# Attention and gated feed-forward on one core: the last 512 queries as two chunks of 256, two key tiles to a score bank, loads and first normalisations reordered

## The chip, the core and the metric

The kernel runs on one core of a Trainium2 chip. A core has five engines that work from queues of their own and meet through semaphores: TensorE (PE, matmuls; its weight loads are shown apart as PEld), VectorE (DVE), ScalarE (ACT), GpSimd (POOL) and SyncE (SP), which here issues the transfers between the main memory and the on-chip memory. Matmuls write to eight score and work banks of 512 float32 per partition; every result is copied out of a bank by ScalarE or VectorE. The metric is the time of one execution on the device, in microseconds (us). Below 0.2% a difference can't be told from none here.

## What is computed

A transformer block on 2048 tokens of width 512, in bfloat16: layer norm, attention with 32 heads of width 16, the output projection and the residual, then layer norm, a gated feed-forward of width 1792 and its residual.

```python
qkv = (x @ wqkv).reshape(B, S, 3, H, Dh).transpose(2, 0, 3, 1, 4)   # of the normalised x; H = 32, Dh = 16
scores = einsum("bhqd,bhkd->bhqk", q, k) * Dh ** -0.5
o = einsum("bhqk,bhkd->bhqd", softmax(scores), v)
h = x + o.transpose(0, 2, 1, 3).reshape(B, S, D) @ wo
h2 = h + (gelu(hn @ w_gate) * (hn @ w_up)) @ w_down                  # hn: h normalised; gelu by tanh; F = 1792
```

## The kernel before, in words

The work is cut by queries into four chunks of 512 (`NCH`). A chunk has eight units (`NSLOT`), each of four heads; a unit runs over 16 key tiles of 128 (`NT`). The smallest piece is a score tile: one head group `g`, one key tile `kt`, 512 queries, which fills one bank. There are 32 units x 16 x 4 = 2048 of them (`TILES`), and they are taken in steps of three and two banks in turn (`SLOTS`, `STEPS`): 819 steps. A step is one set of score matmuls (`qk`; four heads side by side in the array, 32 rows each), then one exponential of ScalarE over the three or two banks (`exps`, L1153 by its helper), whose bfloat16 result goes to a ring of 30 tiles (`PT`). The value matmuls (`pv`) take four tiles at a time and add over the key tiles in one bank (`PVB`), 17 rows per head: 16 values and the denominator. After a unit, `ofin` copies that bank (L1342), transposes it (L1346), inverts the denominators (L1350) and writes the divided result by token (L1353).

When a chunk has its eight units, `post` (four query tiles of 128) transposes them (L1383), copies (L1385), multiplies by `wo`, adds the residual (L1392), takes statistics (L1396, L1397), forms the factor by a power on POOL (L1399, L1400), normalises (L1401) and transposes back (L1405, L1407). Then `gates`, `ups` and `downs` run the feed-forward in 14 blocks of 128 (`NFC`): 56 gate matmuls, 56 up matmuls of 512 columns each, and 56 down matmuls. Chunks 0 to 2 do this under the scores of the next chunk, and their gelu is made of three POOL operations (L1433, L1434, L1435), a tanh on ScalarE between two exponentials (L1441) and VectorE operations. Chunk 3 does it when no scores are left, with the gelu of ScalarE's table (`gelu_tail`, L1447). `check` tests all denominators on VectorE (L1498 to L1504) and sets a flag that could send the kernel to a second path; it isn't taken here.

At the start, `loads` issues the transfers on SP, in order: x of chunk 0 in two halves, the first 128 columns of keys and of queries of `wqkv`, x of chunk 1, values, and so on. `ln1` normalises chunk by chunk: statistics on VectorE (L1213, L1214; for chunk 1 sums on ScalarE, L1199 and L1201), the factor of four tiles by one power on POOL (L1217), then the normalisation of four tiles (L1222), on VectorE for chunk 0 and on POOL for the others. `ln1_T` transposes each tile (L1229) and copies it (L1236, or L1234 on ScalarE). `proj_kq` and `proj_v` make keys, queries and values, and their results are copied by VectorE (L1260, L1270, L1282) and one by ScalarE (L1267).

What sets the order is a planner (`Sched`), run when the kernel is built: each piece of work is a stream with a due time (`prio`), each operation has an assumed duration, and the planner emits, engine by engine, the operation that can start first. On the chip each engine then runs its list strictly in that order. `fill` puts matmuls of zeros (L1513, L1523) where TensorE would pause, by a running count of columns owed (`RATE`, `OWED`); `warm` does so before the first scores (L1510).

## Time and profile before

| | |
|---|---|
| median of 3 runs | 1063.62 us (1062.66 to 1064.13) |
| profiled execution, its own time | 1062.85 us |
| its span, first to last instruction | 1061.1 us |
| granted TensorE clock, mean over the span | 0.990 |
| moved by all transfers | 14.96 MB |

A row of a timeline gives start and duration in us, engine, line, operation, result and operands, shapes and count, and in brackets the idle time before it with what ended it. A row of a group gives line, engine, operation and shapes, then busy us and the mean ns of one, then idle us before and what ended most of it. Rows of neighbouring instructions of one kind are merged, and their durations may overlap.

### The profile page before, as it was taken

The numbers are of one execution on the slowest core, as the hardware profiler recorded it, in microseconds if no ns is written. First come the engines' busy times: TensorE is split into PE (matmuls) and PEld (weight loads), VectorE is DVE, ScalarE is ACT, GpSimd is POOL, SyncE is SP. The second block draws the span as 40 slices with busy tenths as digits, with TensorE's granted clock in tenths as the row PEclk, the third lists the DMA queues.
The fourth block names the chain that finished last, engine by engine and source line by source line (L and its number), as shares of the span: only waits on it lengthen the run. The fifth ranks groups of instructions, "written<-read, shape, count | busy, mean of one in ns | idle before, by whom it ended". The sixth has DMA issues, their size and how long they took to land.

```text
span 1061.1 us, 15019 instructions
## 1 busy us (share of the span) xinstructions
PE 951.1 (90%) x6139; PEld 288.9 (27%) x6255; DVE 258.6 (24%) x462; ACT 971.7 (92%) x897; POOL 181.6 (17%) x191
## 2 busy tenths in 40 slices
...
DMA packets 12847, 14.96 MB, mean 14 GB/s; under 512 B 1760, under 2 KB 11744, under 8 KB 12768
## 3 DMA queue, kind: packets, MB, share of 16 engines
...
q14 instruction: 28, 0.23, 0.1%
...
## 4 chain that ended last, share of the span: by engine, by line
ACT 32%; PE 28%; issue 23%; POOL 12%; DVE 2%; ACTq 0%; POOLq 0%; DVEq 0%
ACT PT L1153 32%; PE pbank L1146 13%; PE pbank L1147 12%; POOL w_sb L1435 5%; POOL w_sb L1433 4%; POOL w_sb L1434 3%; PE pbank L1513 2%; POOL xn_sb L1222 1%; PE pbank L1346 1%; DVE g_sb L1431 0%; DVE QT L1270 0%; DVE stats_93 L1396 0%; ACTq L152 0%; PE pbank L1523 0%; DVE VA L1282 0%
## 5 line engine op out<-in xcount | busy, mean ns | idle before, releaser
L1153 ACT ACTIVATE PT<-pbank 128x1536 bf16<-128x1536 f32 (+1 forms) x819 | 934.1, 1406 | 21.4 <-PE pbank L1147 20.3
L1147 PE MATMUL pbank<-QT,KT 32*128 32x512 bf16 x2048 | 319.5, 386 | 69.6 <-ACT PT L1153 48.6
L1513 PE MATMUL pbank<-ones_bf,zero_bf 128*128 128x512 bf16 x743 | 226.3, 383 | 7.3 <-issue 7.0
L1147 PE MATMUL pbank<-PT,VA 128*17 128x512 bf16 x2048 | 201.0, 385 | 1.2 <-ACT PT L1153 0.4
L1147 PEld LDWEIGHTS pbank<-QT,KT 32*128 32x128 bf16 x2048 | 78.0, 91 | 380.8 <-ACT PT L1153 350.7
L1342 DVE COPY OA<-pbank 128x512 f32<-128x512 f32 x32 | 22.1, 691 | 501.6 <-PE pbank L1147 501.6
L1399 POOL TENSOR_SCALAR rstd_95<-mv_94 128x1 f32<-128x1 f32 x16 | 3.6, 224 | 793.4 <-DVE mv_94 L1397 791.0
L1513 PEld LDWEIGHTS pbank<-ones_bf,zero_bf 128*128 128x128 bf16 x811 | 57.0, 97 | 99.7 <-issue 84.6
L1147 PEld LDWEIGHTS pbank<-PT,VA 128*17 128x17 bf16 x2048 | 49.1, 87 | 118.1 <-issue 109.6
L1146 PE MATMUL pbank<-wd_sb,GUT 128*128 128x512 bf16 x215 | 56.4, 381 | 0.9 <-issue 0.8
L1435 POOL TENSOR_TENSOR w_sb<-w_sb,g_sb 128x512 f32<-128x512 f32 x42 | 56.1, 1336 | 3.5
L1433 POOL TENSOR_TENSOR w_sb<-g_sb 128x512 f32<-128x512 f32 x42 | 45.4, 1080 | 24.8 <-DVE g_sb L1431 24.8
L1442 DVE SCALAR_TENSOR_TENSOR w_sb<-w_sb,g_sb 128x512 f32<-128x512 f32 x42 | 34.8, 827 | 19.5 <-ACT w_sb L1441 19.3
L1146 PE MATMUL pbank<-xnT,wqkv_sb 128*128 128x512 bf16 x121 | 35.5, 394 | 1.0 <-issue 0.5
L1467 DVE SCALAR_TENSOR_TENSOR GUT<-pbank,w_sb 128x512 bf16<-128x512 f32 x42 | 28.9, 690 | 28.4 <-PE pbank L1146 28.2
L1447 ACT ACTIVATE w_sb<-pbank 128x512 f32<-128x512 f32 x14 | 8.4, 598 | 29.9 <-PE pbank L1146 29.9
L1434 POOL TENSOR_SCALAR w_sb<-w_sb 128x512 f32<-128x512 f32 x42 | 34.5, 821 | 3.7
L1431 DVE COPY g_sb<-pbank 128x512 f32<-128x512 f32 x42 | 28.9, 687 | 23.0 <-PE pbank L1146 23.0
L1441 ACT ACTIVATE w_sb<-w_sb 128x512 f32<-128x512 f32 x42 | 27.1, 646 | 7.1 <-POOL w_sb L1435 7.1
L1346 PE MATMUL pbank<-ident_77,OA 128*128 128x128 f32 x128 | 27.3, 298 | 0.9 <-DVE OA L1342 0.9
L1222 POOL TENSOR_SCALAR xn_sb<-x_sb,mv,rstd 128x512 bf16<-128x512 bf16 x12 | 24.8, 2079 | 0.5 <-issue 0.3
L1146 PEld LDWEIGHTS pbank<-wd_sb,GUT 128*128 128x128 bf16 x224 | 17.6, 98 | 26.3 <-issue 12.2
...
## 6 DMA issues: line engine op xcount, KB each, us to landing
...
wu_sb<-in_B_w_up_dram SPq DMA_DIRECT2D x1, 1792.0 KB, 12.4
...
```

Source lines behind the costliest of these rows:

```text
L1146: return lambda e: e.matmul(o, l, r, start=start, stop=stop)
L1147: return lambda e: e.matmul(o, l, r, start=start, stop=stop, tile_position=tile)
L1153: return lambda e: e.activation(out=o, in_=i, func=func, **kw)
L1222: lambda e, t=t: e.tensor_scalar(out=xn_sb[:, t % 8, :], in0=x_sb[:, t, :], scalar1=mv[:, t, 0:1], scalar2=rstd[:, t:t + 1], op0=ALU.subtr ...
L1346: yield Op("pe", 2 * TTR32, cols=256, fns=[lambda e, qt=qt: e.transpose(out=pbank[:, b, 128 * qt:128 * qt + 128], in_=OA[:, par, 128 * qt: ...
L1431: yield Op("dve", 0.61, lambda e: e.tensor_copy(out=gs, in_=pbank[:, b, :]), reads=[("pb", b)], writes=[("g", i)], extra=dE)
L1433: yield Op("pool", 1.05, lambda e: e.tensor_tensor(out=ws, in0=gs, in1=gs, op=ALU.mult), reads=[("g", i)], writes=[("w", i)])
L1434: yield Op("pool", 0.62, lambda e: e.tensor_scalar(out=ws, in0=ws, scalar1=GA, scalar2=1.0, op0=ALU.mult, op1=ALU.add), reads=[("w", i)], ...
L1435: yield Op("pool", 1.27, lambda e: e.tensor_tensor(out=ws, in0=ws, in1=gs, op=ALU.mult), reads=[("w", i), ("g", i)], writes=[("w", i)])
L1442: yield Op("dve", 0.6, lambda e: e.scalar_tensor_tensor(out=ws, in0=ws, scalar=1.0, in1=gs, op0=ALU.add, op1=ALU.mult), reads=[("w", i), ( ...
L1467: fn = lambda e: e.scalar_tensor_tensor(out=GUT[:, fc, :], in0=pbank[:, b, :], scalar=0.5, in1=w_sb[:, i, :], op0=ALU.mult, op1=ALU.mult)
L1513: fill_op = Op("pe", TMM, lambda e: e.matmul(pbank[:, PVB, :], zero_bf[:], ones_bf[:], start=False, stop=False, skip_group_check=True), re ...
```

## The change

The chunks become five: 512, 512, 512, 256, 256 (`CHUNKS`), so 40 units. In a unit of 256 queries a bank still holds 512 columns: two key tiles of 256 queries each, so steps, banks and exponentials stay 819 and as wide as before. `qk` then issues two matmuls of 256 columns for a bank, first the even key tiles of the step, then the odd ones; `pv` issues eight matmuls of 256 columns in place of four of 512. `ofin`, `post`, `gates`, `ups` and `downs` are cut to the chunk's width. The first chunk of 256 keeps the gelu of POOL and tanh, under the scores of the last one; only the last chunk of 256 takes `gelu_tail`. Its h and normalised h lie in the place of chunk 0's.

At the start, all of `wqkv` comes as two transfers behind chunk 1's load of x, and the loads of x for chunks 2 and 3 are behind them. Each tile of `ln1` has its own factor and goes on by itself (`ln1_norm`): chunks 0 and 1 are normalised on VectorE, chunks 2 and 3 on POOL as x times factor plus (minus mean times factor), with two small operations for the second term. All four copies of chunk 0's transposed tiles are on ScalarE. The planner counts a transfer by its megabytes behind the ones before it, some assumed durations differ, `T0` is 12, and `fill` no longer puts a filler ahead of work other than scores and values unless the pause is at least a matmul long. The denominators' array has 640 values per partition, set to one at the start by POOL.

```diff
-            self.t[op.eng] = start + 0.1
-            self.done[tok] = end
+            self.t[op.eng] = start + 0.5
+            self.pipe = max(start + 1.8, self.pipe) + op.dur / 0.36
+            self.done[tok] = self.pipe + 0.3
...
+CHUNKS = (512, 512, 512, 256, 256)
...
+    h_c = [at("h_c%d" % c, [128, CHUNKS[c] // 128, D], BF16, h_off[c][0]) for c in range(NC)]
+    hnT_c = [at("hnT_c%d" % c, [128, 4, CHUNKS[c]], BF16, h_off[c][0] + 4096) for c in range(NC)]
...
-    units = [(c, s) for c in range(NCH) for s in range(NSLOT)]
+    units = [(c, s) for c in range(NC) for s in range(NSLOT)]
     NU = len(units)
-    TILES = [(u, kt, g) for u in range(NU) for kt in range(NT) for g in range(4)]
+
+    def qpart(c):
+
+        q0 = 128 * first_t[c]
+        return q0 // 512, slice(q0 % 512, q0 % 512 + CHUNKS[c])
+
+    TILES = [(u, m, g) for u in range(NU) for m in range(NT * CHUNKS[units[u][0]] // 512) for g in range(4)]
...
-    T0 = 14.0
+    T0 = 12.0
...
-        yield d(x_sb[:, 0:2, :], xv[:, 0:2, :], ("x", 0, 0), [("x", 0, 0)], 3.0)
-        yield d(x_sb[:, 2:4, :], xv[:, 2:4, :], ("x", 0, 1), [("x", 0, 1)], 3.3)
-        yield d(wqkv_sb[:, :, D:D + 128], wv[:, :, D:D + 128], "wk0", ["wk0"], 4.0)
-        yield d(wqkv_sb[:, :, 0:128], wv[:, :, 0:128], "wq0", ["wq0"], 4.0)
+            return d(x_sb[:, 4 * c:4 * c + 4, :], xv[:, 4 * c:4 * c + 4, :], ("x", c), [("x", c)], 0.5)
+        yield d(x_sb[:, 0:2, :], xv[:, 0:2, :], ("x", 0, 0), [("x", 0, 0)], 0.25)
+        yield d(x_sb[:, 2:4, :], xv[:, 2:4, :], ("x", 0, 1), [("x", 0, 1)], 0.25)
         yield xl(1)
-        yield d(wqkv_sb[:, :, 2 * D:3 * D], wv[:, :, 2 * D:3 * D], "wv", ["wv"], 5.0)
+        for hf in range(2):
+            yield d(wqkv_sb[:, 2 * hf:2 * hf + 2, :], wv[:, 2 * hf:2 * hf + 2, :], ("w", hf), [("w", hf)], 0.75)
         yield xl(2)
-        yield d(wqkv_sb[:, :, D + 128:2 * D], wv[:, :, D + 128:2 * D], "wk1", ["wk1"], 5.0)
-        yield d(wqkv_sb[:, :, 128:D], wv[:, :, 128:D], "wq1", ["wq1"], 5.0)
         yield xl(3)
-        yield d(wo_sb[:], A_wo.rearrange("(c p) j -> p c j", p=128), "wo", ["wo"], 8.0)
+        yield d(wo_sb[:], A_wo.rearrange("(c p) j -> p c j", p=128), "wo", ["wo"], 0.5)
...
+        for t in ts_:
+            if c != 1:
                 yield Op("dve", 0.66, lambda e, t=t: e.bn_stats(out=stats[:, t, :], in_=x_sb[:, t, :]), reads=[xkey(c, t)], writes=[("stats", t)])
                 yield Op("dve", 0.1, lambda e, t=t: e.bn_aggr(out=mv[:, t, :], in_=stats[:, t, :]), reads=[("stats", t)], writes=[("mv", t)])
-            yield Op("pool", 0.25, lambda e: e.tensor_scalar(out=rstd[:, sl], in0=mv[:, sl, 1], scalar1=EPS, scalar2=None, op0=ALU.add),
-                     reads=[("mv", t) for t in ts_], writes=[("rstd", c)])
-        yield Op("pool", 1.05, lambda e: e.tensor_tensor(out=rstd[:, sl], in0=rstd[:, sl], in1=nhalf[:, sl], op=ALU.pow),
-                 reads=[("rstd", c), "nhalf"], writes=[("rstd", c)])
-        for t in ts_:
-            eng = "dve" if c == 0 else "pool"
-            yield Op(eng, 0.35 if c == 0 else 0.77,
-                     lambda e, t=t: e.tensor_scalar(out=xn_sb[:, t % 8, :], in0=x_sb[:, t, :], scalar1=mv[:, t, 0:1], scalar2=rstd[:, t:t + 1], op0=ALU.subtract, op1=ALU.mult),
-                     reads=[xkey(c, t), ("rstd", c), ("mv", t)], writes=[("xn", t % 8)], gate=lambda t=t: t < 8 or C.get(("xnT", t - 8), 0))
-            sch.add(ln1_T(c, t), 3 + 7 * c)
+            sch.add(ln1_norm(c, t), 2 + 7 * c)
+
+    def ln1_norm(c, t):
+        tt_ = slice(t, t + 1)
+        if c != 1:
+            yield Op("pool", 0.25, lambda e: e.tensor_scalar(out=rstd[:, tt_], in0=mv[:, t, 1:2], scalar1=EPS, scalar2=None, op0=ALU.add),
+                     reads=[("mv", t)], writes=[("rstd", t)])
+            yield Op("pool", 0.57, lambda e: e.tensor_tensor(out=rstd[:, tt_], in0=rstd[:, tt_], in1=nhalf[:, 0:1], op=ALU.pow),
+                     reads=[("rstd", t), "nhalf"], writes=[("rstd", t)])
+        ok = lambda: t < 8 or C.get(("xnT", t - 8), 0)
+        if c < 2:
+            yield Op("dve", 0.35,
+                     lambda e: e.tensor_scalar(out=xn_sb[:, t % 8, :], in0=x_sb[:, t, :], scalar1=mv[:, t, 0:1], scalar2=rstd[:, tt_], op0=ALU.subtract, op1=ALU.mult),
+                     reads=[xkey(c, t), ("rstd", t), ("mv", t)], writes=[("xn", t % 8)], gate=ok)
+        else:
+            yield Op("pool", 0.2, lambda e: e.tensor_tensor(out=htmp[:, tt_], in0=mv[:, t, 0:1], in1=rstd[:, tt_], op=ALU.mult),
+                     reads=[("mv", t), ("rstd", t)], writes=[("nmr", t)])
+            yield Op("pool", 0.25, lambda e: e.tensor_scalar(out=htmp[:, tt_], in0=htmp[:, tt_], scalar1=-1.0, scalar2=None, op0=ALU.mult),
+                     reads=[("nmr", t)], writes=[("nmr", t)])
+            yield Op("pool", 0.77,
+                     lambda e: e.tensor_scalar(out=xn_sb[:, t % 8, :], in0=x_sb[:, t, :], scalar1=rstd[:, tt_], scalar2=htmp[:, tt_], op0=ALU.mult, op1=ALU.add),
+                     reads=[xkey(c, t), ("rstd", t), ("nmr", t)], writes=[("xn", t % 8)], gate=ok)
+        sch.add(ln1_T(c, t), 2 + 7 * c)
...
-        if c == 0 and t % 2:
-            yield Op("act", 0.47, lambda e: e.activation(out=o_ap, in_=i_ap, func=ACT.Copy), reads=[("pb", b)], writes=[("xnT", t)])
+        if c == 0:
+            yield Op("act", 0.6, lambda e: e.activation(out=o_ap, in_=i_ap, func=ACT.Copy), reads=[("pb", b)], writes=[("xnT", t)])
         else:
-            yield Op("dve", 0.61, lambda e: e.tensor_copy(out=o_ap, in_=i_ap), reads=[("pb", b)], writes=[("xnT", t)])
+            yield Op("dve", 0.42, lambda e: e.tensor_copy(out=o_ap, in_=i_ap), reads=[("pb", b)], writes=[("xnT", t)])
...
-                u, kt, g = TILES[i0 + k]
+                u, m, g = TILES[i0 + k]
                 c, slot = units[u]
-                fns.append(MM(pbank[:, b0 + k, :], KT[32 * g:32 * g + 32, slot // 2, 128 * kt:128 * kt + 128], QT[32 * g:32 * g + 32, c, slot, :], True, True, (32 * g, 0)))
-                rd += [("qT", slot, c), ("kT", slot // 2, kt // 4)]
-            yield Op("pe", TQK, cols=128 * n, fns=fns, reads=sorted(set(rd)), writes=[("pb", b0 + k) for k in range(n)], gate=lambda: C["exp"] >= st - len(SLOTS) + 1)
+                c4, qs = qpart(c)
+                nq = CHUNKS[c]
+                for e in range(512 // nq):
+                    kt = m * (512 // nq) + e
+                    fns.append((e, MM(pbank[:, b0 + k, e * nq:e * nq + nq], KT[32 * g:32 * g + 32, slot // 2, 128 * kt:128 * kt + 128],
+                                      QT[32 * g:32 * g + 32, c4, slot, qs], True, True, (32 * g, 0))))
+                    rd += [("qT", slot, c4), ("kT", slot // 2, kt // 4)]
+            fns = [f for _, f in sorted(fns, key=lambda a: a[0])]
+            yield Op("pe", TQK + 0.05 * (len(fns) > n), cols=128 * n, fns=fns, reads=sorted(set(rd)), writes=[("pb", b0 + k) for k in range(n)], gate=lambda: C["exp"] >= st - len(SLOTS) + 1)
...
-            for kt in range(NT):
+            nq = CHUNKS[c]
+            r = 512 // nq
+            for m in range(NT // r):
                 p = [(4 * n + g) % NRING for g in range(4)]
-                yield Op("pe", TPV, cols=512, fns=[MM(pbank[32 * g:32 * g + 17, PVB, :], VA[:, kt, head(slot, g), :], PT[:, p[g], :], kt == 0, kt == NT - 1, (0, 32 * g))
-                                                   for g in range(4)],
-                         reads=[("V", kt), "VA_ones"] + [("PT", p[g]) for g in range(4)], writes=[("pb", PVB)],
+                fns = [MM(pbank[32 * g:32 * g + 17, PVB, 0:nq], VA[:, kt, head(slot, g), :], PT[:, p[g], (kt % r) * nq:(kt % r) * nq + nq], kt == 0, kt == NT - 1, (0, 32 * g))
+                       for kt in range(m * r, m * r + r) for g in range(4)]
+                yield Op("pe", TPV + 0.05 * (r - 1), cols=512, fns=fns,
+                         reads=[("V", kt) for kt in range(m * r, m * r + r)] + ["VA_ones"] + [("PT", p[g]) for g in range(4)], writes=[("pb", PVB)],
                          gate=lambda: C.get("tiles", 0) >= 4 * n + 4 and C["oa"] >= u)
                 n += 1
                 C["pv"] = n
+                C["open"] = m + 1 < NT // r
...
+        b = yield Acquire(reads=[("OA", par), "ident32"], gate=lambda: c < 2 or C["oproj"] >= first_t[c - 1])
+        for hf in range(nb // 2):
+            yield Op("pe", 2 * TTR32, cols=256, fns=[TR(pbank[:, b, 128 * qt:128 * qt + 128], OA[:, par, 128 * qt:128 * qt + 128], ident32[:]) for qt in (2 * hf, 2 * hf + 1)],
+                     reads=[("OA", par), "ident32"], writes=[("pb", b)])
...
+        for t in range(first_t[c], first_t[c + 1]):
+            yield Op("sp", 0.125, lambda e, t=t: e.dma_start(out=xres[:, t % 4, :], in_=xv[:, t, :]), writes=[("xres", t % 4)], dma=("xres", t % 4),
+                     gate=lambda: C["oproj"] >= first_t[c])
...
+        tail = c == NC - 1
...
-                yield Op("pe", 2 * TMM, cols=1024, fns=[MM(pbank[:, b, :], wg_sb[:, dc, 128 * fc:128 * fc + 128], hT[:, dc, :], dc == 0, dc == 3)
-                                      for dc in (2 * hf, 2 * hf + 1)], reads=rd, writes=[("pb", b)])
+                yield Op("pe", 2 * tmm(nq), cols=2 * nq, fns=[MM(pbank[:, b, 0:nq], wg_sb[:, dc, 128 * fc:128 * fc + 128], hT[:, dc, :], dc == 0, dc == 3)
+                                                              for dc in (2 * hf, 2 * hf + 1)], reads=rd, writes=[("pb", b)])
...
+        if gap < TMM and not any(k[0] == "pb" and k[1] <= PVB for k in nxt.writes):
+            return False```

Where work moves, at the three places that the prediction rests on.

TensorE at the start, from behind the query matmuls to the first scores, before (`xn_sb`: normalised tiles to be transposed; `wqkv_sb,xnT`: values; `xnT,wqkv_sb`: queries and keys; `QT,KT`: scores; in brackets what the instruction waits for):

```order
L1229 MATMUL pbank<-ident,xn_sb 128x128 [waits prog_dve,prog_pool]
L1229 MATMUL pbank<-ident,xn_sb 128x128 x3
L1229 MATMUL pbank<-ident,xn_sb 128x128 [waits prog_dve,prog_pool]
L1229 MATMUL pbank<-ident,xn_sb 128x128 x3
L1229 MATMUL pbank<-ident,xn_sb 128x128 [waits prog_dve,prog_act,prog_pool]
L1229 MATMUL pbank<-ident,xn_sb 128x128 x3
L1146 MATMUL pbank<-xnT,wqkv_sb 128x512 [waits prog_dve,dma_wk0]
L1146 MATMUL pbank<-xnT,wqkv_sb 128x512 x3
L1229 MATMUL pbank<-ident,xn_sb 128x128 [waits prog_dve,prog_pool]
L1229 MATMUL pbank<-ident,xn_sb 128x128 x3
L1147 MATMUL pbank<-QT,KT 128x512 [waits prog_dve]
L1147 MATMUL pbank<-QT,KT 128x512 x4
```

and now, from the first matmuls that wait for the weights:

```order
L1169 MATMUL pbank<-wqkv_sb,xnT 128x512 [waits prog_act,dma_('w', 1),dma_('w', 0)]
L1169 MATMUL pbank<-wqkv_sb,xnT 128x512 x3
L1169 MATMUL pbank<-xnT,wqkv_sb 128x512 [waits prog_act]
L1169 MATMUL pbank<-xnT,wqkv_sb 128x512 x3
L1169 MATMUL pbank<-xnT,wqkv_sb 128x512 [waits prog_dve]
L1169 MATMUL pbank<-xnT,wqkv_sb 128x512 x3
L1169 MATMUL pbank<-wqkv_sb,xnT 128x512 [waits prog_dve,prog_act]
L1169 MATMUL pbank<-wqkv_sb,xnT 128x512
L1170 MATMUL pbank<-QT,KT 128x512 [waits prog_dve]
L1170 MATMUL pbank<-QT,KT 128x512 x4
L1169 MATMUL pbank<-wqkv_sb,xnT 128x512 x2
L1265 MATMUL pbank<-ident,xn_sb 128x128 [waits prog_pool]
```

The transposes that wait for POOL's tiles stood ahead of the first scores; the first such one now stands behind them.

VectorE at the start, from the normalisation of chunk 0 to the copy of the first keys, now (`dma_('x', 2)` is chunk 2's load of x; in the list before, the four normalisations stood behind two statistics with that wait):

```order
L1250 TENSOR_SCALAR xn_sb<-x_sb,mv,rstd 128x512 [waits prog_pool] x3
L1250 TENSOR_SCALAR xn_sb<-x_sb,mv,rstd 128x512 [waits prog_dve,prog_pool]
L1236 BN_STATS stats<-x_sb 128x6 [waits dma_('x', 2)]
L1237 BN_AGGR mv<-stats 128x2 [waits prog_dve]
L1236 BN_STATS stats<-x_sb 128x6
L1317 CAST VA<-pbank 128x32x16 [waits prog_pe]
L1237 BN_AGGR mv<-stats 128x2 [waits prog_dve]
L1236 BN_STATS stats<-x_sb 128x6
L1305 TENSOR_SCALAR QT<-pbank,qmask 128x512 [waits prog_act,prog_pe]
L1295 CAST KT<-pbank 128x512 [waits prog_pe]
```

The normalisations moved ahead of that load; the copy of the first keys is behind it.

TensorE near the end, before (`PT,VA`: values; `ones_bf,zero_bf`: filler):

```order
L1147 MATMUL pbank<-QT,KT 128x512 x3
L1147 MATMUL pbank<-PT,VA 17x512 x4
L1513 MATMUL pbank<-ones_bf,zero_bf 128x512
L1147 MATMUL pbank<-QT,KT 128x512 x2
L1513 MATMUL pbank<-ones_bf,zero_bf 128x512 x3
```

and now, with the first chunk of 256 in its up (`wu_sb`) and down (`wd_sb`) matmuls:

```order
L1170 MATMUL pbank<-QT,KT 128x256 x6
L1169 MATMUL pbank<-hnT_c_72,wu_sb 128x256 x4
L1169 MATMUL pbank<-wd_sb,GUT 128x512 x3
L1170 MATMUL pbank<-QT,KT 128x256 x4
L1170 MATMUL pbank<-PT,VA 17x256 x8
```

A step of three banks has six score matmuls, four tiles of values take eight, and feed-forward work stands where filler stood. The last down matmul of that chunk is followed by four more score sets, then the last chunk's epilogue is left.

147 lines of the change are left out of this document (79 added, 68 removed).

## The prediction

> **What bounds the kernel now.** I read the page's busy shares first, then the groups and the waits of ScalarE, then the timeline of both ends. The first three lines are from the page (share of the span; groups: busy us, mean ns, idle before), the fourth from the waits of ScalarE (us in total, times, longest).
>
> ```profile
> PE 951.1 (90%) x6139; PEld 288.9 (27%) x6255; DVE 258.6 (24%) x462; ACT 971.7 (92%) x897; POOL 181.6 (17%) x191
> L1153 ACT ACTIVATE PT<-pbank 128x1536 bf16<-128x1536 f32 (+1 forms) x819 | 934.1, 1406 | 21.4 <-PE pbank L1147 20.3
> L1513 PE MATMUL pbank<-ones_bf,zero_bf 128*128 128x512 bf16 x743 | 226.3, 383 | 7.3 <-issue 7.0
> ACT PT L1153 <- PE pbank L1147: 20.3, 14, 8.3
> ```
>
> ScalarE is the bound: the 819 exponentials take 934.1 of 1061.1 us, 1.14 each. TensorE's 90% is no second bound, since 226.3 us of it are filler. In the whole run ScalarE waits for scores only 14 times, 20.3 us. So the span is a head (before the first exponential), a row of exponentials that hardly stops, and a tail. The timeline of ScalarE (start, duration, what, count, idle before) shows where that row begins, stalls and ends:
>
> ```profile
> 29.30 2.37 ACT L1153 ACTIVATE PT<-pbank 128x1536 bf16<-128x1536 f32 x2 [8.31 <-PE pbank L1147]
> 33.42 1.45 ACT L1153 ACTIVATE PT<-pbank 128x1536 bf16<-128x1536 f32 x1 [1.75 <-PE pbank L1147]
> 36.32 1.02 ACT L1153 ACTIVATE PT<-pbank 128x1024 bf16<-128x1024 f32 x1 [1.45 <-PE pbank L1147]
> 38.37 2.52 ACT L1153 ACTIVATE PT<-pbank 128x1536 bf16<-128x1536 f32 x2 [1.02 <-PE pbank L1147]
> 42.14 6.89 ACT L1153 ACTIVATE PT<-pbank 128x1536 bf16<-128x1536 f32 x6 [1.25 <-PE pbank L1147]
> 51.62 16.14 ACT L1153 ACTIVATE PT<-pbank 128x1536 bf16<-128x1536 f32 x14 [2.60 <-PE pbank L1147]
> ...
> 998.49 3.93 ACT L1153 ACTIVATE PT<-pbank 128x1536 bf16<-128x1536 f32 x3
> ```
>
> First exponential 29.30, last one done at 998.49 + 3.93 = 1002.42: head 29.3, middle 973.1, tail 58.7. The change does not touch how many exponentials there are, so it can act only by the head, the waits of the middle, and the tail. The profiled execution took 1062.85 us, 1.75 over its span and 0.8 below the median shown (1063.62); the sum is made against 1062.85 and 0.8 is added at the end.
>
> **The tail.** What is left after the last exponential is the last chunk's epilogue: 512 queries now, 256 after. Timeline of the tail:
>
> ```profile
> 1002.92 0.69 DVE L1342 COPY OA<-pbank 128x512 f32<-128x512 f32 x1 [25.04 <-PE pbank L1147]
> 1005.35 1.07 PE L1383 MATMUL pbank<-ident,Otok 128*128 128x128 bf16 x16 [0.16 <-DVE Otok L1353]
> 1005.66 0.69 DVE L1500 TENSOR_TENSOR LCHK<-LCHK,LINV 128x512 f32<-128x512 f32 x1
> 1009.85 0.57 POOL L1400 TENSOR_TENSOR rstd_95<-rstd_95,nhalf 128x1 f32<-128x1 f32 x1
> 1019.42 2.76 PE L1146 MATMUL pbank<-hnT_c_71,wg_sb 128*128 128x512 bf16 x11
> 1043.61 12.25 PE L1146 MATMUL pbank<-wd_sb,GUT 128*128 128x512 bf16 x55
> 1055.89 0.69 DVE L1486 TENSOR_TENSOR out_sb<-pbank,h_c_67 128x512 bf16<-128x512 f32 x1 [2.33 <-PE pbank L1146]
> ```
>
> Four pieces. Up to the gate matmuls 1019.42 - 1002.42 = 17.0; 112 gate and up matmuls back to back 24.2 (0.216 each); 56 down matmuls 12.25; the last output 5.2.
> - Down: 28 in place of 56, same shape: 6.1 saved.
> - Gate and up: the same 112, each 256 columns wide. Bounds: 0.057 (the 16 matmuls of 128 columns in 1.07, with their weight loads) and 0.216 (no gain). Cost goes with columns between these rows (128 columns 0.057, 512 columns 0.216), so 0.110: 12.3, saved 11.9. ScalarE and VectorE, one instruction per block each at 0.6 to 0.7 for 512 columns, get narrower too and stay below the 0.88 that TensorE needs for a block's eight.
> - Up to the gates: copy of the outputs 0.69 to some 0.42, two transposes fewer (0.6), the multiplication half as long: the token transposes start 2.1 after the last exponential in place of 2.9. Two query tiles now go through projection, statistics, power (0.57) and transposes, not four. The check of the denominators costs more (640 values for 512; 0.69 becomes 0.86) and stands ahead of the first copies on VectorE, its last reduction behind them. Following that queue: copies done at 4.2, reduction 5.0, first sum 5.7, its statistics 6.5, POOL 7.4, normalised 8.3; the second tile 1.5 behind at 9.8, its transposes and copy at 10.7. So gates at 10.75, not 17.0: 6.25 saved.
>
> Tail 34.4 in place of 58.7: **24.3 saved** (12.4 if the gate and up matmuls gain nothing).
>
> **The head.** Rows: three of the table by stretch (busy us of each engine, then clock, DMA share, GB/s), the timeline, and three groups of VectorE.
>
> ```profile
> 0.00:5.00 5.00, 3.26 (x8) 1.19 (x9) 2.35 (x8) 1.28 (x1) 3.68 (x10) 1.00 0.50 139
> 5.00:10.00 5.00, 3.80 (x15) 1.42 (x13) 1.94 (x6) 1.75 (x5) 1.28 (x2) 1.00 1.01 324
> 10.00:12.00 2.00, 0.00 (x0) 0.00 (x0) 0.80 (x3) 1.91 (x7) 0.00 (x0) 1.00 1.10 337
> 8.18 0.63 ACT L1199 ACTIVATE sqj<-x_sb 128x512 bf16<-128x512 bf16 x1 [6.11 <-DMA x_sb<-in_A_x_dram]
> 11.17 0.69 DVE L1213 BATCH_NORM_STATS2 stats<-x_sb 128x6 f32<-128x512 bf16 x1 [4.12 <-DMA x_sb<-in_A_x_dram]
> 12.79 1.35 DVE L1222 TENSOR_SCALAR xn_sb<-x_sb,mv,rstd 128x512 bf16<-128x512 bf16 x4
> 16.08 8.28 POOL L1222 TENSOR_SCALAR xn_sb<-x_sb,mv,rstd 128x512 bf16<-128x512 bf16 x4 [0.19 <-POOL rstd L1217]
> 28.65 1.03 PE L1147 MATMUL pbank<-QT,KT 32*128 32x512 bf16 x5
> L1270 DVE TENSOR_SCALAR QT<-pbank,qmask 128x512 bf16<-128x512 f32 x31 | 23.1, 749 | 6.5 <-PE pbank L1146 5.7 <-PE pbank L1147 0.2
> L1282 DVE CAST VA<-pbank 128x512 bf16<-128x512 f32 x16 | 11.1, 694 | 20.4 <-PE pbank L1146 20.4
> L1260 DVE CAST KT<-pbank 128x512 bf16<-128x512 f32 x16 | 11.1, 691 | 15.7 <-PE pbank L1146 15.5
> ```
>
> Before, two queues hold the first scores back. On VectorE the four normalisations of chunk 0 stand behind statistics that wait for chunk 2's load of x (11.17), and start only at 12.79. Then TensorE, in order, has five tiles of POOL's slow normalisation (8.28 for four) ahead of the first scores at 28.65. After, chunk 0's normalisations stand ahead of that load, chunk 1's are on VectorE, and no transpose that needs chunk 1 or 2 is ahead of the first scores.
>
> What is late next: the key copy on VectorE, now behind three tiles' statistics of chunk 2. Loads: 0.695 MB had moved by 5.0 (139 GB/s), then 0.324 and 0.337 MB per us. Before, 1.31 MB were queued up to chunk 1's load of x, and 1.73 had moved when it was there (8.18): loads behind it had taken 0.41. The new queue has 1.05 MB up to that load, 2.62 up to the weights, 3.15 up to chunk 2's load of x. With no such share taken they land at 6.1, 10.9 and 12.5, with 0.41 at 7.4, 12.1 and 13.7; I take the middle, 6.7, 11.5, 13.1. ScalarE then has two tiles' statistics (3.0), four copies (2.3): transposed tiles at 12.0, query and key matmuls (8) by 14, its own query copy and another tile's statistics by 16.2, so it is not last. VectorE from 13.1: statistics 0.83 + 0.83 + 0.73, value copy 0.69, query copy 0.75, key copy 0.69: 17.6. Scores to exponential took 0.65 at half clock: first exponential 18.2 (17.6 to 18.9) in place of 29.3, **11.1 saved**.
>
> The waits behind it. Until 43 there were four, 5.5 in all, at the pace of POOL's tiles. After, chunk 1's tiles come from VectorE once POOL has its factors (18.8 to 20.2) and VectorE its statistics (20.0); the third score step then waits some 1.1. Chunks 2 and 3 stay on POOL in another form. Groups of POOL:
>
> ```profile
> L1434 POOL TENSOR_SCALAR w_sb<-w_sb 128x512 f32<-128x512 f32 x42 | 34.5, 821 | 3.7
> L1222 POOL TENSOR_SCALAR xn_sb<-x_sb,mv,rstd 128x512 bf16<-128x512 bf16 x12 | 24.8, 2079 | 0.5 <-issue 0.3 <-POOL rstd L1217 0.2
> L1400 POOL TENSOR_TENSOR rstd_95<-rstd_95,nhalf 128x1 f32<-128x1 f32 x16 | 9.1, 572 | 1.3
> ```
>
> The new normalisation is multiply and add, the pair of operations of the 0.82 row; its types and per-row factors are those of the 2.08 row (subtract and multiply). I take 0.82: the size is the same in both rows, and the arithmetic is what the change alters. A tile then costs 0.57 + 0.82 and three small ones of 0.22 with gaps, 2.3; its twin at 2.08 costs 3.6. At 2.3 tile 11 is ready about 26 and tile 15 about 35, as the exponentials come to need them; at 3.6, up to 10 us late. Saved: 4.4 at best, a loss of 6 at worst; with the later waits (2.60 at 51.62) unchanged and some of the first lot likely to return, I take **2 saved**.
>
> **The middle.** Chunk 3's feed-forward (256 queries) leaves the tail and runs under the last scores: 14 tanh between exponentials (the 14 gelus of the tail are in the tail sum). Group, and wait for POOL (us, times, longest):
>
> ```profile
> L1441 ACT ACTIVATE w_sb<-w_sb 128x512 f32<-128x512 f32 x42 | 27.1, 646 | 7.1 <-POOL w_sb L1435 7.1
> ACT w_sb L1441 <- POOL w_sb L1435: 7.1, 17, 0.6
> ```
>
> At 256 columns between 0.32 and 0.65, say 0.48; records of ScalarE overlap by 1.406 - 1.14 = 0.27; waiting adds 7.1 / 42 = 0.17. So 14 x 0.38 = **5 lost** (3 to 11). TensorE's share of that work, 18 us (112 x 0.11 + 28 x 0.216), displaces filler.
>
> The last 512 queries need 1024 score and 1024 value matmuls of 256 columns for 512 each of 512. If the load of the second round's weights is covered, columns are equal and it costs nothing; if not, one load per round. Timeline rows of TensorE:
>
> ```profile
> 41.70 0.60 PE L1147 MATMUL pbank<-QT,KT 32*128 32x512 bf16 x5
> 78.41 0.61 PE L1147 MATMUL pbank<-PT,VA 128*17 128x512 bf16 x8
> 221.27 0.39 PE L1147 MATMUL pbank<-QT,KT 32*128 32x512 bf16 x2 [0.22 <-ACT PT L1153]
> 221.59 0.39 PE L1147 MATMUL pbank<-PT,VA 128*17 128x512 bf16 x4
> ```
>
> One round is 0.39, two of the same kind are 0.60 and 0.61: the second adds only its stream of 0.216, its loads are covered. Changing kind costs 0.32 from start to start (221.27 to 221.59), so an uncovered load is 0.10. A 256 column stream of 0.11 still covers 0.10, barely: I take **0**, and 0.10 per round as the other end.
>
> Sum: 1062.85 - 24.3 - 11.1 - 2 + 5 = 1030.5, and 0.8 to the median: **1031**.
>
> **Rivals.**
> - *POOL's tiles stay at 2.08.* For it: types and factors of that row. Against: the 0.82 row. The waits then give back 6 where I have 2 saved: 1039.
> - *Half-width matmuls are not half as long.* For it: no row has 256 columns. At 0.16 each the tail keeps 5.6 more, and a partly uncovered load in each of 205 last score steps some 3: 1040.
> - *Chunk 3's feed-forward is not covered.* TensorE has little filler left where a feed-forward runs, so its 18 us push the scores: 1049. Against: the few waits of ScalarE for scores in such stretches.
> - *Slower: TensorE sets the pace for the last 512 queries.* Place: the 205 score steps whose banks take two key tiles. Every step pays an uncovered load for scores (0.10) and 2.5 / 4 of one for values (0.06), and once TensorE ends last each third step adds the 0.22 after the exponential seen at 221.27: 0.23 x 205 = 47, so 1031 + 47 = 1078. It decides from 32 / 205 = 0.16 per step. Against: the rows of 0.60 and 0.61. [...]
>
> **How the numbers follow.** Forecast 0.60, POOL 0.17, half-width 0.13, uncovered 0.05, slower 0.05. The forecast's own range is 1025 to 1037 (waits 4.4 saved and 3 lost for tanh, or none saved and 9 lost). The range 1024 to 1045 takes in the first two rivals and leaves out the last two. A difference under 0.2% is about what a measurement here can't tell from none; the near end of the slower rival falls there: faster 0.93, same 0.02, slower 0.05.
>
> **What would show it.** First exponential near 18; chunk 2's load of x by 13.1; POOL's normalisation near 0.82; gates some 10.8 after the last exponential, 112 matmuls in 12.3, downs 6.1; no rise of ScalarE's waits for scores in the last quarter beyond the 14 tanh. Wrong, if the first exponential is past 24, the tail over 42, or ScalarE waits at most of the last 205 steps.

## The result, and the profile after

The changed kernel takes 1028.34 us (median of 4 runs, 1027.24 to 1029.05), the kernel before 1063.14 beside it: a ratio of 0.967, with an interval of 0.9654 to 0.9687. The forecast was 1031. The profiled execution took 1028.30 us, its span is 1026.6.

The page of the changed kernel (first line: busy time, share and instructions of each engine; second: the exponentials), and ScalarE's waits (us in total, times, longest):

```profile
PE 947.2 (92%) x7310; PEld 295.7 (29%) x7310; DVE 277.4 (27%) x530; ACT 974.7 (95%) x913; POOL 197.3 (19%) x264
L1176 ACT ACTIVATE PT<-pbank 128x1536 bf16<-128x1536 f32 (+1 forms) x819 | 937.7, 1349 | 10.0 <-PE pbank L1170 8.3
```

```profile
ACT PT L1176 <- PE pbank L1170: 8.3, 14, 3.0
ACT w_sb L1495 <- POOL w_sb L1488: 6.1, 16, 0.5
```

The exponentials are as many as before and as long (937.7 us busy, before 934.1); ScalarE waits 8.3 us for scores, before 20.3. The timeline of ScalarE shows both ends of the row of exponentials, the one large wait, and two tanh of 256 and one of 512 columns between exponentials:

```profile
18.48 6.88 ACT L1176 ACTIVATE PT<-pbank 128x1536 bf16<-128x1536 f32 x6 [0.60 <-PE pbank L1170]
28.34 15.01 ACT L1176 ACTIVATE PT<-pbank 128x1536 bf16<-128x1536 f32 x13 [2.97 <-PE pbank L1170]
...
286.41 0.68 ACT L1495 ACTIVATE w_sb<-w_sb 128x512 f32<-128x512 f32 x1
286.93 2.42 ACT L1176 ACTIVATE PT<-pbank 128x1024 bf16<-128x1024 f32 x2
...
962.29 0.52 ACT L1495 ACTIVATE w_sb<-w_sb 128x256 f32<-128x256 f32 x1
962.59 3.81 ACT L1176 ACTIVATE PT<-pbank 128x1536 bf16<-128x1536 f32 x3
...
971.54 20.74 ACT L1176 ACTIVATE PT<-pbank 128x1024 bf16<-128x1024 f32 x18
```

The first exponential starts at 18.48, the last ends at 971.54 + 20.74 = 992.28. So, beside the kernel before:

| | before | after | difference |
|---|---|---|---|
| head, up to the first exponential | 29.3 | 18.5 | -10.8 |
| middle, to the end of the last | 973.1 | 973.8 | +0.7 |
| tail | 58.7 | 34.3 | -24.4 |
| span | 1061.1 | 1026.6 | -34.5 |

The tail on TensorE, gate and down matmuls:

```profile
1002.82 1.48 PE L1169 MATMUL pbank<-hnT_c_73,wg_sb 128*128 128x256 bf16 x12
...
1015.06 6.21 PE L1169 MATMUL pbank<-wd_sb,GUT 128*128 128x512 bf16 x28
```

Gate matmuls start 10.5 after the last exponential (before 17.0), 112 gate and up matmuls take 1015.06 - 1002.82 = 12.2 (24.2), 28 down matmuls 6.2 (12.25).

The head, in the order in which things wait for each other: chunk 1's x is there (first row, where the statistics of its first tile start), two tiles' statistics, copies of chunk 0's transposed tiles, TensorE's third tile, chunk 2's x (fifth row), key copy, scores; then the next key copy and the score matmuls behind the wait of 2.97:

```profile
7.80 0.63 ACT L1220 ACTIVATE sqj<-x_sb 128x512 bf16<-128x512 bf16 x1 [5.72 <-DMA x_sb<-in_A_x_dram]
10.70 1.06 ACT L1270 ACTIVATE xnT<-pbank 128x512 bf16<-128x512 bf16 x2
11.42 0.58 PE L1265 MATMUL pbank<-ident,xn_sb 128*128 128x128 bf16 x4 [2.50 <-ACT xnT L1270]
13.08 1.85 PE L1169 MATMUL pbank<-wqkv_sb,xnT 128*128 128x512 bf16 x4
13.29 0.69 DVE L1236 BATCH_NORM_STATS2 stats<-x_sb 128x6 f32<-128x512 bf16 x1 [4.52 <-DMA x_sb<-in_A_x_dram]
17.29 0.68 DVE L1295 CAST KT<-pbank 128x512 bf16<-128x512 f32 x1
18.05 0.60 PE L1170 MATMUL pbank<-QT,KT 32*128 32x512 bf16 x5
...
27.16 0.69 DVE L1295 CAST KT<-pbank 128x512 bf16<-128x512 f32 x1
27.91 0.60 PE L1170 MATMUL pbank<-QT,KT 32*128 32x512 bf16 x5
```

At the end of those 2.50 us of waiting TensorE's clock fell: the table by stretches of 2 us (busy time of PE, PEld, DVE, ACT, POOL, then granted clock, share and GB/s of the transfers) has it at half speed for some 3.4 us (0.83, 0.50 and 0.82 are 0.7, 2.0 and 0.7 us at 0.5), and the four matmuls of 13.08 take 1.85 for it (1.02 in the run without the filler rule below, where the clock is 1.00).

```profile
8.00:10.00 2.00, 0.92 (x7) 0.31 (x5) 0.55 (x2) 1.94 (x6) 0.32 (x1) 1.00 1.01 389
10.00:12.00 2.00, 0.58 (x5) 0.56 (x6) 0.00 (x0) 1.73 (x5) 0.00 (x0) 0.83 1.06 370
12.00:14.00 2.00, 2.00 (x10) 0.93 (x8) 0.69 (x1) 1.70 (x4) 0.00 (x0) 0.50 1.10 354
14.00:16.00 2.00, 2.00 (x9) 0.69 (x8) 1.79 (x5) 0.99 (x5) 1.30 (x5) 0.82 0.31 100
```

POOL's normalisation in its new form, from the groups of POOL, and two rounds of 256 columns in the timeline of TensorE:

```profile
L1258 POOL TENSOR_SCALAR xn_sb<-x_sb,rstd,htmp 128x512 bf16<-128x512 bf16 x8 | 6.3, 789 | 1.0 <-issue 0.3
```

```profile
985.56 0.39 PE L1170 MATMUL pbank<-QT,KT 32*128 32x256 bf16 x6
985.89 0.40 PE L1170 MATMUL pbank<-PT,VA 128*17 128x256 bf16 x8
```

Six score matmuls of 256 columns take 0.39, as three of 512 do, and the next kind of work starts 0.33 later.

### The profile page after: what moved, and what is told of

The parts are those of the page before. It is cut to its first block, busy times and chain, and to the rows that moved or that the text cites. A ratio compares the mean times of both kernels' runs of the same rounds, so it can differ in the third digit from the quotient of the medians.

```text
span 1026.6 us, 17429 instructions
## 1 busy us (share of the span) xinstructions
PE 947.2 (92%) x7310; PEld 295.7 (29%) x7310; DVE 277.4 (27%) x530; ACT 974.7 (95%) x913; POOL 197.3 (19%) x264
## 4 chain that ended last, share of the span: by engine, by line
ACT 39%; PE 31%; issue 17%; POOL 10%; DVE 2%; DMA 1%; ACTq 0%; SPq 0%; DVEq 0%; POOLq 0%
ACT PT L1176 38%; PE pbank L1170 14%; PE pbank L1169 11%; POOL w_sb L1488 4%; PE pbank L1567 4%; POOL w_sb L1486 3%; POOL w_sb L1487 3%; PE pbank L1577 1%; PE pbank L1173 1%; ACT w_sb L1495 1%; DMA x_sb<-in_A_x_dram 1%; DVE g_sb L1484 1%; PE pbank L1265 0%; ACT sqj L1220 0%; ACT sqj L1222 0%
## 5 line engine op out<-in xcount | busy, mean ns | idle before, releaser
L1176 ACT ACTIVATE PT<-pbank 128x1536 bf16<-128x1536 f32 (+1 forms) x819 | 937.7, 1349 | 10.0 <-PE pbank L1170 8.3
L1170 PE MATMUL pbank<-QT,KT 32*128 32x512 bf16 (+1 forms) x2560 | 318.1, 340 | 62.9 <-ACT PT L1176 44.7
L1170 PE MATMUL pbank<-PT,VA 128*17 128x512 bf16 (+1 forms) x2560 | 199.9, 340 | 0.9 <-ACT PT L1176 0.6
L1170 PEld LDWEIGHTS pbank<-QT,KT 32*128 32x128 bf16 x2560 | 81.7, 91 | 367.9 <-ACT PT L1176 334.5
L1389 DVE COPY OA<-pbank 128x512 f32<-128x512 f32 (+1 forms) x40 | 23.3, 583 | 415.2 <-PE pbank L1170 415.2
L1170 PEld LDWEIGHTS pbank<-PT,VA 128*17 128x17 bf16 x2560 | 51.0, 87 | 119.0 <-issue 109.5
L1486 POOL TENSOR_TENSOR w_sb<-g_sb 128x512 f32<-128x512 f32 (+1 forms) x56 | 53.8, 962 | 72.7 <-DVE g_sb L1484 72.7
L1488 POOL TENSOR_TENSOR w_sb<-w_sb,g_sb 128x512 f32<-128x512 f32 (+1 forms) x56 | 66.2, 1183 | 4.7
L1169 PE MATMUL pbank<-wd_sb,GUT 128*128 128x512 bf16 x224 | 59.2, 382 | 0.1
L1496 DVE SCALAR_TENSOR_TENSOR w_sb<-w_sb,g_sb 128x512 f32<-128x512 f32 (+1 forms) x56 | 42.5, 758 | 39.3 <-ACT w_sb L1495 39.0
L1484 DVE COPY g_sb<-pbank 128x512 f32<-128x512 f32 (+1 forms) x56 | 34.8, 621 | 44.9 <-PE pbank L1169 42.0
L1487 POOL TENSOR_SCALAR w_sb<-w_sb 128x512 f32<-128x512 f32 (+1 forms) x56 | 40.8, 729 | 4.9
L1522 DVE SCALAR_TENSOR_TENSOR GUT<-pbank,w_sb 128x512 bf16<-128x512 f32 (+1 forms) x56 | 34.6, 620 | 24.3 <-PE pbank L1169 23.8
L1495 ACT ACTIVATE w_sb<-w_sb 128x512 f32<-128x512 f32 (+1 forms) x56 | 34.3, 613 | 6.2 <-POOL w_sb L1488 6.1
L1169 PE MATMUL pbank<-xnT,wqkv_sb 128*128 128x512 bf16 x128 | 35.9, 383 | 0.0
L1577 PE MATMUL pbank<-ones_bf,zero_bf 128*128 128x512 bf16 x99 | 29.5, 383 | 1.4 <-DVE Otok L1400 0.9
L1173 PE MATMUL pbank<-ident_79,OA 128*128 128x128 f32 x128 | 26.1, 296 | 0.4 <-DVE OA L1389 0.3
L1305 DVE TENSOR_SCALAR QT<-pbank,qmask 128x512 bf16<-128x512 f32 x31 | 23.1, 750 | 9.5 <-PE pbank L1169 8.6
L1169 PEld LDWEIGHTS pbank<-wd_sb,GUT 128*128 128x128 bf16 x224 | 17.0, 97 | 24.9 <-issue 12.6
```

The source lines that it names most:

```text
L1169: return lambda e: e.matmul(o, l, r, start=start, stop=stop)
L1170: return lambda e: e.matmul(o, l, r, start=start, stop=stop, tile_position=tile)
L1173: return lambda e: e.transpose(out=o, in_=i, identity=idn)
L1176: return lambda e: e.activation(out=o, in_=i, func=func, **kw)
L1484: yield Op("dve", 0.61, lambda e: e.tensor_copy(out=gs, in_=pbank[:, b, 0:nq]), reads=[("pb", b)], writes=[("g", i)], extra=dE)
L1486: yield Op("pool", 1.05, lambda e: e.tensor_tensor(out=ws, in0=gs, in1=gs, op=ALU.mult), reads=[("g", i)], writes=[("w", i)])
```

## The experiments

All medians stand beside runs of the kernel before on the same chip; those were 1063.14 to 1064.35, so times of different groups compare by their ratio to it. Differences in us below are of medians; by the ratios a kernel stands up to 1.8 us better beside the changed one. The edits are shown shortened. Head, middle and tail are cut as in the table above.

**The split alone.** Loads, first statistics and first normalisations of before, with the split, the two-key-tile banks and the new filler rule:

```diff
-    T0 = 12.0
+    T0 = 14.0
     # loads, ln1, ln1_T, proj_kq, proj_v, ffn_loads: as in the kernel before
```

> Only the split of the queries into 512, 512, 512, 256, 256 (with the two key tiles to a score bank and the new rule for filler), and the loads, the statistics and the normalisation of before. Theory (head, waits and tail add up, the split's price is 14 tanh): the first exponential stays near 29.3, the part after the last exponential falls from 58.7 to about 34.3, the middle grows by 5; 1063 - 24.4 + 5 = 1044 us (1041 to 1047). Rival (weights of the second key tile are not hidden): the middle grows by 12 or more and the kernel stays over 1050. Rival (filler rule or order of loads carries part of the gain): the tail falls by clearly less than 24.

Measured: 1044.14 us, ratio 0.982 (0.980 to 0.984). From ScalarE's timeline:

```profile
29.69 2.37 ACT L1175 ACTIVATE PT<-pbank 128x1536 bf16<-128x1536 f32 x2 [8.30 <-PE pbank L1169]
...
986.96 20.74 ACT L1175 ACTIVATE PT<-pbank 128x1024 bf16<-128x1024 f32 x18
```

Head 29.7, tail 1042.0 - 1007.7 = 34.3, middle 978.0, 4.9 more than before. The tail's 24.4 come from this half alone. The 4.9 in the middle are near the 5 forecast, but they are not the split's price by itself, since the filler rule and other edits to the planning count in them too (see the next run and the filler rule below).

**The head alone.**

```diff
-CHUNKS = (512, 512, 512, 256, 256)
+CHUNKS = (512, 512, 512, 512)
```

> The changed kernel with four chunks of 512 queries: only the loads, the pipelined first tiles and the new form on GpSimd are left of the change. Theory: first exponential near 18.5, waits for scores behind it near 7.7 as in the changed kernel, no price of a split, tail 58.7 as before; 1063 - 10.8 - 4.3 = 1048 us (1045 to 1051). Rival (head and tail are not independent, a part of the head's gain comes back in the middle): over 1052.

Measured: 1044.74 us, ratio 0.982 (0.980 to 0.984), 3 less than expected and just under the range of 1045 to 1051.

```profile
17.19 6.88 ACT L1176 ACTIVATE PT<-pbank 128x1536 bf16<-128x1536 f32 x6 [1.74 <-PE pbank L1170]
...
939.25 45.59 ACT L1176 ACTIVATE PT<-pbank 128x1024 bf16<-128x1024 f32 x40
```

Head 17.2, middle 984.84 - 17.19 = 967.7 (5.5 less than before), tail 57.9. The spans of the two halves save 19.1 and 18.4, together 3.0 more than the whole change: 0.9 of that is the head (1.3 earlier here, with no dip of the clock and chunk 1's x at 6.70 for 7.80, less the 0.4 by which the split alone started later), 1.3 the middle and 0.8 the tail. Some edits stand in both halves (the filler rule, a few assumed durations and gates of the planner), so what they give is counted twice in that sum; they were not run by themselves. The rival doesn't hold: nothing of the head's gain came back. This run also prices the split: counted from the first exponential, its row is the same as the changed kernel's up to the 614th within 0.05 us, and then the changed kernel falls behind, 973.8 - 967.7 = 6.1 in the middle.

**POOL in its old form.**

```diff
-            yield Op("pool", 0.2, ... htmp = mean * rstd
-            yield Op("pool", 0.25, ... htmp = htmp * -1
-            yield Op("pool", 0.77, ... xn = x * rstd + htmp      (mult, add)
+            yield Op("pool", 0.77, ... xn = (x - mean) * rstd    (subtract, mult)
```

> The changed kernel with one edit: GpSimd normalises the tiles of chunks 2 and 3 with subtract and multiply in one instruction, as before, and not with multiply and add after two small instructions. Theory (the pair of operations sets the time): 2.08 us for each of the eight instructions where it is 0.79 now, eight tiles 8 us later in all, ScalarE waits 3 to 8 us more; 1031 to 1036 us. Rival (the place of the instruction, or what else uses the memory at that time, sets it): it stays near 0.8 and the time at 1028. Second rival: 2.08 each, but the transposed tiles are not needed that early, and the time stays at 1028.

Measured: 1037.99 us, ratio 0.975 (0.9735 to 0.9772), 9.6 over the changed kernel. The groups of POOL, and the waits in ScalarE's timeline:

```profile
L1254 POOL TENSOR_SCALAR xn_sb<-x_sb,mv,rstd 128x512 bf16<-128x512 bf16 x8 | 16.7, 2086 | 0.9 <-issue 0.3
```

```profile
33.67 6.88 ACT L1176 ACTIVATE PT<-pbank 128x1536 bf16<-128x1536 f32 x6 [7.20 <-PE pbank L1170]
43.76 6.89 ACT L1176 ACTIVATE PT<-pbank 128x1536 bf16<-128x1536 f32 x6 [3.21 <-PE pbank L1170]
```

The same tiles cost 2086 ns in the one form and 789 in the other. Which of the two operations, or the source of the mean, makes the difference was not separated. With 2.09 the waits grow by more than expected: 2.97 becomes 7.20, and a second of 3.21 appears. This one form is worth 9.6 us, more than the two microseconds that the forecast booked for all waits together.

**A second split.**

```diff
-CHUNKS = (512, 512, 512, 256, 256)
+CHUNKS = (512, 512, 256, 256, 256, 256)
```

> The changed kernel with the third 512 queries split as well: 512, 512, 256, 256, 256, 256. The tail is the same, so it shows the price of one more split by itself. Theory (rounds of 256 columns cost nothing, 14 more tanh cost 5): 1028 + 5 = 1033 us (1031 to 1036), tail 34.3. Rival (each two-key-tile bank pays an uncovered load of weights, 0.16 or more a step over 205 more steps): 1045 or more, with ScalarE waiting for scores at many of these steps.

Measured: 1026.93 us, ratio 0.9647 (0.9631 to 0.9664): not 5 slower, but 1.4 us less than the changed kernel by the medians (the intervals overlap). The expectation, 1031 to 1036, was wrong in its count. The third chunk's 14 tanh of 512 columns are gone, and 28 of 256 are there; ScalarE's groups by shape:

```profile
L1495 ACT ACTIVATE w_sb<-w_sb 128x256 f32<-128x256 f32 x42 | 21.1, 502 | 0.0
L1495 ACT ACTIVATE w_sb<-w_sb 128x512 f32<-128x512 f32 x28 | 18.2, 649 | 4.9 <-POOL w_sb L1488 4.9
```

From start to start a tanh of 512 holds the exponentials up for 0.52 (286.41 to 286.93), one of 256 for 0.30 (962.29 to 962.59): 28 x 0.30 - 14 x 0.52 = 1.1 more, and 1.2 less waiting for POOL (4.9 for 6.1). The middle is 971.7, 2.1 shorter than the changed kernel's. About 1.0 of it is a wait for scores at 688.43 in the changed kernel, behind a lump of filler (next run), which is not there with the third chunk split; what is left of that was not settled. For uncovered weight loads the run is a clear no: 205 more steps with two rounds, and nothing lost.

**The filler rule.**

```diff
-        if gap < TMM and not any(k[0] == "pb" and k[1] <= PVB for k in nxt.writes):
-            return False
```

> The changed kernel without the two lines that hold filler back when the next work of TensorE does not write a score or value bank. Theory (filler lies in gaps that nothing waits for): 1028 us, within 1.5. Rival (these lines are part of the saved waits): 2 us or more slower, with longer waits of ScalarE for scores.

Measured: 1024.97 us, ratio 0.9632 (0.9615 to 0.9648): 3.4 faster without the two lines. The theory was wrong, filler is not free. One of the places, TensorE in the changed kernel around 230 us (L1577: filler; L1173: the transposes after a unit; L1170: scores), and what ScalarE saw of it there and at two places more:

```profile
228.29 0.39 PE L1577 MATMUL pbank<-ones_bf,zero_bf 128*128 128x512 bf16 x1
228.57 0.66 PE L1173 MATMUL pbank<-ident_79,OA 128*128 128x128 f32 x4
229.06 1.46 PE L1577 MATMUL pbank<-ones_bf,zero_bf 128*128 128x512 bf16 x6
230.45 0.60 PE L1170 MATMUL pbank<-QT,KT 32*128 32x512 bf16 x5
```

```profile
230.89 15.01 ACT L1176 ACTIVATE PT<-pbank 128x1536 bf16<-128x1536 f32 x13 [0.72 <-PE pbank L1170]
...
387.97 141.57 ACT L1176 ACTIVATE PT<-pbank 128x1536 bf16<-128x1536 f32 x125 [0.72 <-PE pbank L1170]
...
688.43 103.73 ACT L1176 ACTIVATE PT<-pbank 128x1536 bf16<-128x1536 f32 x91 [0.72 <-PE pbank L1170]
```

and, for the first of them, without the rule:

```profile
227.85 0.44 PE L1173 MATMUL pbank<-ident,OA 128*128 128x128 f32 x2 [0.21 <-DVE OA L1389]
228.13 0.38 PE L1577 MATMUL pbank<-ones_bf,zero_bf 128*128 128x512 bf16 x1
228.60 0.39 PE L1170 MATMUL pbank<-QT,KT 32*128 32x512 bf16 x3
```

The rule refuses filler ahead of work other than scores and values where the pause is short, the columns owed pile up, and the planner pays them in a lump of six matmuls (1.4 us) just ahead of the next score matmuls. Without it, filler stands in ones and twos between the transposes and nothing waits: from 198.74 on ScalarE has 75 exponentials without a gap. The same lump of six stands ahead of the other two waits (386.14 and 686.60). From start to start each of the three costs 1.1, 3.3 in all; without the rule none of them is there, while a new wait of 1.16 stands at 977.81. The middle is 970.8, 3.0 shorter. The other 0.9 is the head (first exponential 17.58): its instructions are in the same order, so that part is the landing of the loads (chunk 2's x at 13.07 for 13.29) and the clock of this execution (1.00 from 8 to 18, worth 0.7), not the rule.

**The order of the loads.**

```diff
         yield d(x_sb[:, 2:4, :], ...)
+        yield wk0, wq0                  # 128 columns each
         yield xl(1)
-        for hf in range(2): yield w(hf) # all of wqkv
+        yield wv
         yield xl(2)
+        yield wk1, wq1
```

> The changed kernel with the order and the slices of the loads of before: chunk 0's key and query columns of the weights ahead of chunk 1's x, chunk 2's x ahead of most weights. Theory (the head is set by two queues, VectorE's and TensorE's, and by when chunk 2's statistics may start on VectorE): chunk 2's x lands near 11.2 in place of 13.3, first exponential 17 to 19, later weights come later; 1028 us, within 2. Rival (the new order of loads carries the head's gain): first exponential past 21 and the time over 1031.

Measured: 1030.16 us, ratio 0.968 (0.9664 to 0.9696), which the interval doesn't tell from the changed kernel's 0.967. The profile does: chunk 2's x is there at 11.67, 1.6 earlier, and yet the first exponential starts at 19.98, 1.5 later. Chunk 1's x came at 8.64 in place of 7.80, the clock fell here as well (0.56 and 0.59 in 12 to 16), and VectorE's query copy, which waits for TensorE's query by way of ScalarE's copy, is at 16.83, no earlier than the 16.63 of the changed kernel. Behind it the order that the planner now made has a value copy (17.50) and a tile's statistics (18.19) ahead of the key copy (18.79), which in the changed kernel follows the query copy at once (17.29). So 1.3 of the 1.5 are order on VectorE's queue, not the landing of a load. The expectation of 17 to 19 missed that; the rival, past 21, doesn't hold either.

**Chunk 1's statistics shared.** Two tiles on ScalarE, two on VectorE; then all four on VectorE:

```diff
+NACT = 2          # then 0
-            if c != 1:
+            if c != 1 or t >= 4 + NACT:     # statistics on VectorE
```

> The changed kernel with chunk 1's statistics shared: two tiles on ScalarE, two on VectorE, which stands idle 8.8 to 13.3. Theory (the wait of 2.97 before the exponential at 28.34 comes from chunk 1's keys, whose tiles wait until ScalarE has done all four tiles' statistics at 17.9): chunk 1's tiles are normalised by 15, the wait goes, first exponential at 18 or a little earlier; 1025 us (1023.5 to 1026.5). Rival (VectorE's copies behind the transposes of chunks 2 and 3 set that wait): no change, 1028.

> The changed kernel with all of chunk 1's statistics on VectorE and none on ScalarE. Theory: the copies of chunk 0's transposed tiles no longer stand behind two tiles' statistics on ScalarE (TensorE waited 2.50 for one of them at 11.42), so key and query matmuls start when the weights are there, near 11.8 in place of 13.1; first exponential near 17, and chunk 1's keys come in time; 1023 us (1021 to 1026). Rival (VectorE becomes the late queue of the head, with four tiles' statistics more, 3.4 us): first exponential 18.5 or later, 1028 or more.

Measured: 1030.45 us, ratio 0.9683 (0.9667 to 0.9699), and 1032.03 us, ratio 0.9689 (0.967 to 0.9708); neither interval tells the run from the changed kernel. With two tiles each:

```profile
19.87 13.73 ACT L1177 ACTIVATE PT<-pbank 128x1536 bf16<-128x1536 f32 x12 [2.54 <-PE pbank L1171]
34.58 8.24 ACT L1177 ACTIVATE PT<-pbank 128x1536 bf16<-128x1536 f32 x7 [0.98 <-PE pbank L1171]
```

The wait of 2.97 is gone, as the theory said: twelve exponentials in a row. But chunk 1's normalised tiles, ready earlier, are transposed ahead of the first scores, whose key copy moves from 17.29 to 18.70, with two of their normalisations and two of their copies ahead of it on VectorE (13.73 to 16.87); the first exponential is 1.4 later, and two later waits (0.98, and 2.42 at 45.23) give back what was won. With all four on VectorE the first exponential is at 19.61, the clock falls twice (0.64 and 0.51 in 12 to 16, 0.50 in 20 to 26), and ScalarE waits for scores 15.6 us in all, nearly twice the changed kernel's 8.3. The rival's numbers held, but not its reason: VectorE is not the late queue, it waits 1.29 and 1.80 us ahead of the key copy (18.41). TensorE waits 2.35 for the weights, to 12.31, and then runs at half clock.

**Chunk 1's keys ahead of chunk 2's transposes.**

```diff
-        b = yield Acquire(reads=[("xn", t % 8), "ident"])
+        b = yield Acquire(reads=[("xn", t % 8), "ident"], gate=lambda: c != 2 or C.get("k1"))
```

> The changed kernel with one rule more: the transposes of chunk 2 wait until the key matmuls of chunk 1 are in TensorE's queue; statistics and everything else as in the changed kernel. Theory (the wait of 2.97 before the seventh exponential is a matter of order: chunk 1's key copy stands behind chunk 2's transposes and their copies): first exponential unchanged near 18.5, the key copy of chunk 1 on VectorE moves from 27.2 to 25 or earlier, the wait falls to about 1, 1026 us (1025 to 1027.5). Rival (chunk 1's statistics are too late by themselves): the wait stays at 2.5 or more, no change.

Measured: 1032.30 us, ratio 0.9705 (0.969 to 0.9721), 4 slower. VectorE's key copy and the wait behind it:

```profile
28.26 0.69 DVE L1297 CAST KT<-pbank 128x512 bf16<-128x512 f32 x1 [0.17 <-PE pbank L1169]
```

```profile
29.55 6.88 ACT L1176 ACTIVATE PT<-pbank 128x1536 bf16<-128x1536 f32 x6 [4.11 <-PE pbank L1170]
```

With chunk 2's transposes held back, the planner filled the free banks with three value blocks, whose copies stood ahead of chunk 1's tiles on VectorE: the key copy came at 28.26, not earlier, and the wait grew. So of the wait of 2.97, it is shown that earlier statistics remove it and that this rule doesn't; an order that removes it without a new wait was not found.

**The clock.** Nine matmuls more of warming up where TensorE had stood idle:

```diff
-            yield Op("pe", 0.25, lambda e: e.matmul(...),
+            yield Op("pe", 0.25, fns=[lambda e: e.matmul(...)] * (4 if 18 <= n <= 20 else 1),
```

> The changed kernel with nine more matmuls that warm TensorE up, of 512 columns, ahead of the transposes of chunk 0's third tile, where TensorE stood idle for 2.50 us in the profile of the changed kernel (8.9 to 11.4) and the granted clock fell to 0.50 right behind it (11.3 to 14.7). Theory (the idle time lets the clock fall, and half a clock makes the query and key matmuls late): clock 1.00 from 10 to 16 us in the profile, first exponential near 17.5 in place of 18.48, 1027 us, 1.1 under the changed kernel. Rival (the clock falls for another reason, or the loads of x set the head): clock 0.5 as before, or first exponential 18 or later, and no change.

Measured: 1027.64 us (1027.22 to 1028.06), ratio 0.9664 (0.965 to 0.9677), 0.7 less, which the intervals don't resolve. The profile does; stretch, VectorE, ScalarE:

```profile
10.00:12.00 2.00, 1.93 (x15) 0.85 (x13) 0.00 (x0) 1.92 (x6) 0.00 (x0) 1.00 1.06 382
12.00:14.00 2.00, 1.87 (x8) 0.71 (x8) 0.88 (x3) 1.90 (x6) 0.00 (x0) 1.00 1.10 349
```

```profile
13.09 0.69 DVE L1236 BATCH_NORM_STATS2 stats<-x_sb 128x6 f32<-128x512 bf16 x1 [4.31 <-DMA x_sb<-in_A_x_dram]
16.40 0.68 DVE L1295 CAST KT<-pbank 128x512 bf16<-128x512 f32 x1
```

```profile
17.59 6.88 ACT L1176 ACTIVATE PT<-pbank 128x1536 bf16<-128x1536 f32 x6 [1.39 <-PE pbank L1170]
```

The clock stays at 1.00, and from chunk 2's x to the key copy it is 3.31 us in place of 4.00 (13.29 to 17.29): the dip cost 0.7. In the changed kernel the half clock lasted 3.41 us (11.32 to 14.73), and in a stretch just as long ahead of it (7.91 to 11.32) TensorE was busy 1.01 us. How little work makes the clock fall, and over what time, was not shown.

**Together.** First the second split, the old filler rule, the warming up and the rule on chunk 1's keys:

> What the runs so far speak for, together: 512, 512, 256, 256, 256, 256 queries, filler by the rule of before, the nine matmuls more of warming up, and chunk 1's key matmuls ahead of chunk 2's transposes. If their effects add up (2.5 for filler, 1.4 for the split of the third 512, 1 for the clock, 2 for the order of the keys, each under the changed kernel's 1028): 1021 us (1019.5 to 1023). If the split and the filler rule save the same stalls, 1023 to 1024.

Measured: 1026.14 us, ratio 0.9651 (0.9635 to 0.9666). The rule on the keys spoils it: first exponential at 17.39, but waits of 3.88 and 4.25 behind it. Without that rule:

```diff
-CHUNKS = (512, 512, 512, 256, 256)
+CHUNKS = (512, 512, 256, 256, 256, 256)
-        if gap < TMM and not any(k[0] == "pb" and k[1] <= PVB for k in nxt.writes):
-            return False
     # and the nine matmuls of warming up
```

> The three edits that gained, without the rule on chunk 2's transposes: 512, 512, 256, 256, 256, 256 queries, filler by the rule of before, and the nine matmuls more of warming up. The stalls behind the first exponential are those of the changed kernel again (one of 2.97 in place of two of 3.88 and 4.25). If the effects add up (first exponential 0.9 earlier, filler 3 in the middle, split 2.4 in the middle): 1028.3 - 6.3 = 1022 us. If the filler rule and the split of the third 512 save the same stalls: 1024 us, no better than the filler rule alone.

Measured: 1021.10 us (1020.43 to 1022.31), ratio 0.9596 (0.9583 to 0.9609): the fastest of all, some 7 us under the changed kernel.

```profile
18.60 6.88 ACT L1176 ACTIVATE PT<-pbank 128x1536 bf16<-128x1536 f32 x6 [1.23 <-PE pbank L1170]
...
963.15 22.91 ACT L1176 ACTIVATE PT<-pbank 128x1024 bf16<-128x1024 f32 x20
```

The middle is 986.06 - 18.60 = 967.5, 6.3 shorter than the changed kernel's: more than the filler rule's 3.0 and the split's 2.1 together, though about 1.0 of these is the same lump of filler, counted in both. ScalarE's tanh wait 2.9 us for POOL here, 6.1 in the changed kernel, which may be the rest; that was not followed further. The head was no shorter in this profile, at a clock of 1.00, since chunk 2's x came at 14.10; the key copy followed at 17.41, again 3.31 later.

## Why the prediction was right, and where it was not

- **The tail: right in every piece.** Gates 10.5 after the last exponential (forecast 10.75), 112 matmuls in 12.2 (12.3), downs 6.2 (6.1), 34.3 in all (34.4). The price of a matmul of 256 columns, taken between rows of 128 and 512, was right (12.2 / 112 = 0.109; forecast 0.110). The split alone shows the same tail.
- **Two rounds to a bank at no cost: right.** 0.39 for six score matmuls of 256 columns, 0.33 to the next kind. The rival in which TensorE sets the pace has no row for it: in the last quarter (740 to 1000) ScalarE waits for scores 4 times, 1.4 us in all, and a second split adds 205 such steps and loses nothing. Why the second round's weight loads cost nothing was not shown.
- **The head: right in size (10.8 for 11.1), its chain right, two terms off in opposite ways.** VectorE's queue behind chunk 2's x sets the first scores, as forecast. In four executions with a full clock the key copy follows that load by 3.31 or 3.32 (12.69 to 16.00, 13.07 to 16.39, 13.09 to 16.40, 14.10 to 17.41) and the first exponential follows the copy by 1.19. The forecast had 5.1 from the load to the first exponential, measured 4.50; the profiled execution has 5.19, since the clock fell. The dip itself, 0.7, was no term of the sum, and the bound of 7.4 for chunk 1's x was too tight: 6.70 to 8.63 in these runs.
- **The waits behind the head: mis-sized.** Forecast 2 saved; measured 12.0 before (20.3 - 8.3) and 7.7 after (8.3 - 0.6), 4.3 saved, the best case of the forecast. The wait of 1.1 for chunk 1's tiles, put at the third step, did not occur; one of 2.97 did, at the seventh exponential, the first whose scores need chunk 1's keys, and the forecast had not followed those keys to their copy on VectorE (27.16). Sharing the statistics removes it.
- **POOL's normalisation: right.** 789 ns (forecast 0.82), a tile every 2.4 to 2.5 us (23.43, 25.84, 28.30; forecast 2.3). The rival at 2.08 was real: the run in the old form costs 1038.0, where the rival said 1039.
- **Tanh: right, the price of the split a little low.** Forecast 5 for 14 more; from the rows 14 x 0.30 = 4.2, and counted in the trace from start to start over all 14, with what some of them waited, 4.9. The whole price of the split in the middle, beside the run of the head alone, is 6.1. The middle grew by only 0.7: these 6.1, less the 4.2 by which it is shorter than in the split alone (978.0 - 973.8), less 1.2 from edits that both halves share.
- **The term left out: the filler rule.** The forecast treated the two lines as free, and they cost 3.0 in the middle. What stands against it was not booked either: the first 100 exponentials of the split alone, with the loads and normalisations of before, are 3.1 shorter than before (122.95 us from the first start to the start of the one after the hundredth, before 126.06, counted in the traces). It is not the filler rule that gains there, for without it the changed kernel has 118.89, with it 118.72; which of the other edits it is was not separated.

The sum came out 2.7 too high (1031 for 1028.3). The waits, 2.3 better than booked, are most of it; the rest is the 0.8 added at the end for the median, which the changed kernel doesn't show (profiled 1028.30, median 1028.34), less 0.2 from head and tail and 0.2 by which the forecast was rounded down. That the sum is so near is in part luck, since terms cancel that were not booked: a rule that cost 3.0, a gain of 3.1 in the first 100 exponentials, a dip of the clock of 0.7, and a chain from load to exponential that is 0.6 shorter than worked out.
